# Windowed attention with block summaries and two feed-forward layers: batch 0's keys and value sums loaded in 4-row and 2-row runs by half of the heads, softmax by pairs of heads, and another order of the work

## The chip, the cores and the metric

One core of one Trainium2 chip. The metric is the device time of one launch in microseconds (us), the median of the runs shown; less is better.

## The reference, cut to what matters

```python
# q, k, v: 2 batches x 8 heads x 768 tokens x 64, float32
block, window = (32, 16)
k_sum = k.reshape(B, H, nb, block, D).max(axis=3)     # 24 summaries per head
v_sum = v.reshape(B, H, nb, block, D).mean(axis=3)
scores_l = scale * q @ k.T, kept where |i - j| < 16
scores_s = scale * q @ k_sum.T + log(32)
a = softmax over [scores_l, scores_s]
x = a @ [v, v_sum]             # 1536 tokens x 512
h = x @ w_in;  x = relu(h)**2 @ w_out           # layer 0: 512 -> 2048 -> 512
h = x @ w_in2; out = h * sigmoid(1.702 * h) @ w_out2    # layer 1: 512 -> 2048 -> 512
```

The weights are float64 in memory (8 bytes each), q, k and v float32.

## The kernel before, in words

**Tiling.** Attention works on blocks of 128 tokens: six of batch 0 (blocks 0 to 5), six of batch 1. q and k come in units of 256 tokens (two blocks) through SyncE's DMA queue (`load_unit`, L374). A "packed" unit puts two consecutive tokens on one partition, so that DMA reads runs of 512 bytes; an unpacked one reads runs of 256 bytes. TensorE transposes a unit against an identity (`transposed`, L462, four 128x128 transposes per PSUM bank at L473), and ScalarE or VectorE copies the bank to `kw` or `qT` (`copy`, L309 on ScalarE, L310 on VectorE). For keys (`t_k`, L488) VectorE takes the maximum of every 32 tokens (L502), GpSimd copies 16-token edges between neighbouring blocks (L509), and when all three units of a batch are there `put_ks` (L518) copies the 24 summaries beside each block's keys (L523). So no block of batch 0 can be scored before all of its keys have landed. The value sums (`sum_v`, L438) are matmuls with a band matrix (L452) over all 768 tokens; `put_vs` (L418) puts them beside the value windows `vw` (`load_vw`, L398: 80 or 96 partitions, runs of 256 bytes).

**One block.** `head` (L534) issues the 16 score matmuls of all eight heads (64x64 tiles, L551; the trace shows each as two), VectorE scales and masks each head and takes its maximum (L565), ScalarE does the exponentials of the four even, then of the four odd heads (L574), GpSimd or VectorE adds 1e-9 (L578), VectorE takes the reciprocal (L588), and VectorE or GpSimd multiplies (L581). `tail` (L593) transposes the result (L602), copies it (`pT`), multiplies with `vw` (L614) and splits the sum into a high and a low part `xh` (L309 or L310) and `xl` (L627).

**Layers.** `fetch` (L684) loads 128 columns of `w_in` (L690) or 128 rows of `w_out` (L694), half a megabyte each, and turns float64 into float32 (L699, L703, L706); `parts` splits that into a high part (L730 or L731) and a low part (L735). `step` (L757) issues the first product of one column group (L768) for 256 or 512 tokens, `finish` (L808) the second (L820).

**Order.** Nothing is ordered by the hardware alone: the string `ORDER` lists tasks (`k,2,1` loads unit 2 of k packed, `tk`, `tq` transpose, `h,i,e` and `t,i` are head and tail of block i, `w,f,z` prepares half of a weight group, `s,f,hf` is a step on 256 tokens, `S,f` on 512), and `Plan` places each operation at its planned start on its engine and emits all by it. `Plan.fill` puts `warm` matmuls (L1123), whose result nobody reads, into the planned gaps of TensorE until the accumulator bank `acc3` is first written.

The line that decides when the layers may begin is the read list of a step:

```python
op("PE", 0.682 * fr + (0.018 if fr < 1 else 0), g1,
   reads=[(wih, 0), (wil, 0)] + [(x[t], (kc, b)) for x in (xh, xl) for b in blks], writes=[(hp, 0)])
```

A step on 256 tokens waits for `xh` and `xl` of two blocks and for the two parts of its weights.

Of the kernel before, what the change touches and what calls it, by code (L numbers as in the profile page):

```python
# [19 lines left out]
NEG = -8.0e9  # L20

# [6 lines left out]
    m,1 k,2,1 sel w,1,0 m,0 k,1,1 q,1,1 k,0,1 tk,0 tk,1 tk,2 pk,0 q,0,1 sv,0 tq,0 h,1,0 tq,1 m,2 h,1,1 h,0,0  # L28
    w,1,1 pk,1 q,2,0 v,0 h,0,1 ps,0 h,3,0 tq,2 v,1 t,1 h,2,0 v,2 v,3 pk,2 h,2,1 t,0 h,3,1 k,3,0 t,2 s,1,0
    t,3 tk,3 w,2,0 q,3,0 tq,3 k,4,1 tk,4 w,3,0 h,4,0 s,1,1 w,3,1 h,5,0 s,3,0 k,5,0 s,3,1 w,5,0 h,5,1 w,2,1  # L30
    w,0,0 q,4,1 s,2,0 tk,5 w,5,1 S,5 w,9,0 s,2,1 w,6,0 h,4,1 pk,3 w,9,1 v,4 S,9 w,6,1 pk,5 tq,4 w,0,1 t,4
    v,5 h,7,0 w,7,0 s,0,0 t,5 w,7,1 s,0,1 w,4,0 S,7 q,5,1 w,11,0 pk,4 w,4,1 h,6,0 sv,1 S,4 h,7,1 v,6 ps,1
    w,8,0 w,11,1 tq,5 v,7 t,7 S,6 h,6,1 w,10,0 h,8,0 v,8 S,11 h,9,0 h,8,1 t,6 w,8,1 h,9,1 v,9 v,10 w,15,0
    t,8 S,8 w,10,1 S,10 w,12,0 w,12,1 w,15,1 v,11 t,9 h,10,0 w,13,0 S,12 S,15 w,14,0 h,11,0 w,13,1 h,10,1
    S,13 w,14,1 h,11,1 t,10 S,14 t,11
# [220 lines left out]
def kernel(  # L256
# [73 lines left out]
    consts = Buf([], None)  # L330

# [32 lines left out]
    kw_ring = ring(attn, "kw", 4, [P, NPAIR, 2, KW])  # L364
# [12 lines left out]
    def load_unit(dst, src, ring_, u, packed):  # L377
        b, j = divmod(u, NU)
        buf = ring_.take()
        if packed:  # L380
            plan.dma(1.85, lambda: nc.sync.dma_start(
                out=buf.t.rearrange("p (h r d) -> p h r d", h=H, r=2),
                in_=src[b, :, j * UNIT:(j + 1) * UNIT, :].rearrange("h (p r) d -> p h r d", r=2)), writes=[(buf, 0)])
# [77 lines left out]

    def transposed(src, dst):  # L462
# [4 lines left out]
        for n in range(2):  # L467
            ps = banks.take()

            def go(n=n, ps=ps):  # L470
                for a in range(4):
                    c0 = (2 * a + n) * P if packed else (a % 2) * H * D + (2 * n + a // 2) * P
                    nc.tensor.transpose(ps.t[:, a * P:(a + 1) * P], buf.t[:, c0:c0 + P], ident)  # L473

            op("PE", 0.46, go, reads=[(buf, 0), (consts, "ident")] + ([] if packed else [(buf, 1)]), writes=[(ps, 0)])
            if not packed:
                copy(lambda n=n: at(slice(0, P), slice(2 * n, 2 * n + 2)),
                     lambda ps=ps: ps.t.rearrange("p (a i t) -> p a i t", a=2, i=2), ps, [(w, ("own", 2 * n))])
                w.writer["own", 2 * n + 1] = plan.ops[-1]
                continue  # L480
            for i in range(2):
                copy(lambda n=n, i=i: at(slice(n * D, n * D + D), slice(0, NPAIR)).rearrange(
                    "p a z (t i) -> p a z t i", i=2)[:, :, :, :, i],
                     lambda ps=ps, i=i: ps.t[i * D:i * D + D, :].rearrange("p (a z t) -> p a z t", a=4, z=2),
                     ps, [(w, ("own", 2 * n + i))], cost=0.59)

    OWNS = [("own", x) for x in range(4)]

    def t_k(u):
# [5 lines left out]
        zero = [(0, NSUM)] if j == 0 else [(1, OWN + P)] if j == NU - 1 else []  # L495
        for i, c0 in zero:
            op("POOL", 0.2, lambda i=i, c0=c0: nc.gpsimd.memset(w.t[:, :, i, c0:c0 + EDGE], 0.0),
               writes=[(w, (i, "l" if c0 == NSUM else "r"))])
        transposed(kin[u], (w, lambda rows, ps: w.t[rows, ps, :, OWN:OWN + P]))
        for z in range(2):  # L500
# [4 lines left out]
               reads=[(w, x) for x in (OWNS if kin[u][1] else OWNS[2 * z:2 * z + 2])], writes=[(ks[b], (j, z))])  # L505
        R = OWN + P

        def edge(dst, di, d0, src, si, s0, side):
            op("POOL", 0.22, lambda: nc.gpsimd.tensor_copy(  # L509
                out=dst.t[:, :, di, d0:d0 + EDGE], in_=src.t[:, :, si, s0:s0 + EDGE]),  # L510
               reads=[(src, x) for x in OWNS], writes=[(dst, (di, side))], port=True)
# [23 lines left out]
    def head(i, e):  # L535
# [5 lines left out]
        if e == 0:  # L541
            both = [banks.take()]
            both.append(banks.take(both[0]))
            sms[i] = sm_ring.take(), st_ring.take()

            def mm():
                for p in range(NPAIR):
                    for c in range(2):
                        k0 = c * (KW - NK)
                        for x in range(2):  # L550
                            nc.tensor.matmul(  # L551
                                both[x].t[c * HALF:(c + 1) * HALF, p * NK:(p + 1) * NK],
                                lhsT=qt.t[x * D:(x + 1) * D, p, z * P + c * HALF:z * P + (c + 1) * HALF],
                                rhs=w.t[x * D:(x + 1) * D, p, z, k0:k0 + NK],
                                start=True, stop=True,
                            )

            op("PE", 0.98, mm, reads=[(w, (z, "l")), (w, (z, "r")), (w, ("s", 0)), (w, ("s", 1))]
               + [(x, y) for x in (w, qt) for y in OWNS], writes=[(both[0], 0), (both[1], 0)])
        s, st = sms[i]  # L560
        for x in range(2 if e == 0 else 0):
            def mx(x=x):
                for p in range(NPAIR):
                    h = 2 * p + x
                    nc.vector.tensor_tensor_reduce(  # L565
                        out=s.t[:, h, :], in0=both[x].t[:, p * NK:(p + 1) * NK], in1=mk, scale=-SCALE, scalar=3.0e38,
                        op0=ALU.add, op1=ALU.min, accum_out=st.t[:, 0, h:h + 1],
                    )

            op("DVE", 0.87, mx, reads=[(both[x], 0), (consts, ("mask", mi))], writes=[(s, x), (st, (0, x))])  # L570

        def ex(e=e):
            for h in range(e, H, 2):
# [583 lines left out]
```

## Time and profile before

| | |
|---|---|
| median of 3 runs | 587.07 us (586.4 to 587.27) |
| span of the profiled execution | 584.6 us |
| TensorE busy | 571.6 us, 98% of the span |
| VectorE, ScalarE, GpSimd busy | 480.4, 441.8, 65.8 us |
| TensorE granted clock | full in all 40 slices |
| first layer step (L768) starts | 36.18 us |

The time of a launch holds the span and about 2.5 us around it (587.07 against 584.6). A share of busy time is an average: the span has an opening, where TensorE has little of its own to do and runs fillers, and the rest, where it hardly pauses. A matmul's shown end is modelled; starts are what shows the pace. A float32 matmul appears as two records, a float32 transpose as one.

### The profile page before, as it was taken

To read this page: it belongs to the slowest core of one execution; us is meant where nothing else is said; L and a number is where in the kernel's file an instruction comes from. 1 tells how busy PE (TensorE), PEld (TensorE's weight loads), DVE (VectorE), ACT (ScalarE), POOL (GpSimd) and SP (SyncE) were. 2 spreads that over 40 slices of the span, in tenths; PEclk is the share of its full clock that TensorE was granted. 3 is DMA by queue.
4 is the path that set the end of the run, shared out by engine and by line. 5 is a ranking of instruction groups with operands and counts; after the bars stand their busy time and mean duration, and the time that the engine had idled before them with its cause. 6 is when DMAs were issued, how large, how long until landed. Compare 5 with 4: busy or idle time off the path is not lost.

```text
span 584.6 us, 9824 instructions
## 1 busy us (share of the span) xinstructions
PE 571.6 (98%) x3440; PEld 474.3 (81%) x3440; DVE 480.4 (82%) x1040; ACT 441.8 (76%) x909; POOL 65.8 (11%) x125
## 2 busy tenths in 40 slices
PE   7899999999999999999999999999999999999997
PEld 6789888788878888888888888888878888888885
DVE  4899998799889998878888899899998898877421
ACT  5899889999888658888888867676587777778322
POOL 5323113112100000100000000000100002000000
PEclk9999999999999999999999999999999999999999
DMA  9999889555446624444444546633465455545001
GB/s 251 238 237 239 243 260 255 148 172 180 148 148 191 201 71 143 143 145 145 145 145 143 180 145 211 186 112 104 148 181 177 152 178 174 178 163 200 0 1 72
DMA packets 87505, 95.79 MB, mean 164 GB/s; under 512 B 29504, under 2 KB 74560, under 8 KB 87456
## 3 DMA queue, kind: packets, MB, share of 16 engines
q1 hardware_dynamic: 87264, 94.78, 54.1%
q0 software_dynamic: 192, 0.39, 0.4%
q8 instruction: 27, 0.44, 0.3%
q14 instruction: 22, 0.18, 0.1%
HBM read 91.62 MB, written 3.15 MB: 162 GB/s over the span
## 4 chain that ended last, share of the span: by engine, by line
PE 86%; ACT 5%; DVE 4%; DMA 3%; SPq 1%; issue 1%; POOL 0%; DVEq 0%; ACTq 0%
PE acc L996 13%; PE acc L820 13%; PE acc L822 11%; PE m L996 10%; PE m L822 9%; PE h L768 6%; PE m L820 6%; PE h L996 3%; PE acc L768 3%; PE m L768 3%; PE h L822 3%; PE h L820 2%; ACT sm L574 2%; PE m L614 2%; DMA kin<-in_k_dram 1%; DMA kin<-in_v_dram 1%
## 5 line engine op out<-in xcount | busy, mean ns | idle before, releaser
L730 ACT CAST w<-xw 128x512 fp32r<-128x512 f32 (+1 forms) x167 | 97.9, 602 | 20.1 <-DVE xw L706 12.8
L735 DVE TENSOR_TENSOR w<-xw,w 128x512 fp32r<-128x512 f32 (+1 forms) x163 | 107.5, 672 | 5.9 <-ACT w L730 4.0
L706 DVE SCALAR_TENSOR_TENSOR xw<-raw,xw 128x512 uint32<-128x512 uint32 x148 | 101.5, 695 | 5.6 <-ACT raw L699 1.8
L699 ACT ACTIVATE raw<-raw 128x512 f32<-128x512 f32 x148 | 96.1, 675 | 10.9 <-DMA raw<-in_moe_w_out_dram 6.3
L820 PE MATMUL acc<-gh,w 128*128 128x512 f32 (+1 forms) x288 | 82.3, 369 | 0.4 <-DVE w L735 0.2
L703 DVE TENSOR_SCALAR xw<-raw 128x512 uint32<-128x512 uint32 x148 | 65.8, 449 | 6.2 <-DMA raw<-in_moe_w_out_dram 5.8
L820 PEld LDWEIGHTS acc<-gh,w 128*128 128x128 f32 x288 | 51.7, 188 | 9.9 <-DVE w L735 0.5
L822 PE MATMUL acc<-w,gh 128*128 128x512 f32 x192 | 59.1, 389 | 0.0
L768 PE MATMUL h<-xh,w 128*128 128x512 f32 (+1 forms) x184 | 55.6, 363 | 0.6 <-DVE st L588 0.6
L820 PE MATMUL acc<-gl,w 128*128 128x512 f32 (+1 forms) x144 | 52.7, 366 | 0.0
L996 PE MATMUL acc<-top,w 128*128 128x512 f32 x192 | 48.3, 391 | 0.0
L822 PE MATMUL m<-w,gh 128*128 128x512 f32 x148 | 45.7, 390 | 0.0
L735 DVE TENSOR_TENSOR gl<-gs,gh 128x512 fp32r<-128x512 f32 x32 | 22.1, 691 | 28.5 <-ACT gh L730 27.8
L730 ACT CAST gh<-gs 128x512 fp32r<-128x512 f32 x32 | 19.9, 622 | 33.5 <-PE acc L822 25.4
L735 POOL TENSOR_TENSOR w<-xw,w 128x512 fp32r<-128x512 f32 x17 | 22.9, 1344 | 195.9 <-ACT w L730 170.2
L996 PEld LDWEIGHTS acc<-top,w 128*128 128x128 f32 x192 | 35.8, 188 | 8.5 <-ACT r L309 1.2
L822 PEld LDWEIGHTS acc<-w,gh 128*128 128x128 f32 x192 | 36.0, 188 | 7.5
L768 PEld LDWEIGHTS h<-xh,w 128*128 128x128 f32 x184 | 33.3, 189 | 6.3 <-ACT sm L574 0.8
L822 PE MATMUL acc<-w,gl 128*128 128x512 f32 x96 | 37.4, 389 | 0.0
L574 ACT ACTIVATE sm<-sm,st 128x120 f32<-128x120 f32 x96 | 36.6, 383 | 0.0
L996 PE MATMUL m<-top,w 128*128 128x512 f32 x138 | 35.0, 391 | 0.0
L996 PE MATMUL acc<-xh,w 128*128 128x512 f32 x100 | 34.0, 389 | 0.0
(188 smaller groups left out, 1201.8 us busy)
## 6 DMA issues: line engine op xcount, KB each, us to landing
raw<-in_moe_w_out_dram SPq DMA_DIRECT2D x88, 512.0 KB, 3.8
raw<-in_moe_w_in_dram SPq DMA_DIRECT2D x60, 512.0 KB, 3.9
vw<-in_v_dram SPq DMA_DIRECT2D x20, 192.0 KB, 5.8
kin<-in_v_dram SPq DMA_DIRECT2D x6, 512.0 KB, 7.0
out_dram<-r SPq DMA_DIRECT2D x12, 256.0 KB, 2.1
kin<-in_k_dram SPq DMA_DIRECT2D x4, 512.0 KB, 6.0
qin<-in_q_dram SPq DMA_DIRECT2D x4, 512.0 KB, 7.1
qin<-in_q_dram SPq DMA_DIRECT2D x4, 256.0 KB, 6.8
```

The source lines that it names most:

```text
L574: nc.scalar.activation(out=s.t[:, h, :], in_=s.t[:, h, :], func=AF.Exp, bias=st.t[:, 0, h:h + 1], scale=-1.0, accum_out=st.t[:, 1, h:h + 1])
L614: nc.tensor.matmul(ps.t[e * D:(e + 1) * D, p * P + c * HALF:p * P + (c + 1) * HALF], lhsT=vw[i].t[:, c, h * D:(h + 1) * D], rhs=t.t[:, h, ...
L699: nc.scalar.activation(out=top, in_=top, func=AF.Prelu, scale=-(2.0 ** -80), alpha=-(2.0 ** -32))
L703: op("DVE", 0.36, lambda: nc.vector.tensor_scalar(out=x.t, in0=raw.t[:, :, 0], scalar1=29, scalar2=None, op0=ALU.logical_shift_right), rea ...
L706: op("DVE", 0.64, lambda: nc.vector.scalar_tensor_tensor(out=x.t, in0=raw.t[:, :, 1], scalar=3, in1=x.t, op0=ALU.logical_shift_left, op1=A ...
L730: plan.soonest([("ACT", 0.09 + 0.44 * fr, False, lambda: nc.scalar.copy(out=hi.t[:, hc], in_=src())), ("DVE", 0.05 + 0.4 * fr, True, lambd ...
L735: eng.tensor_tensor(out=lo.t[:, lc], in0=src(), in1=hi.t[:, hc].bitcast(F32), op=ALU.subtract)
L768: nc.tensor.matmul(hp.t[:, cols], lhsT=w.t[:, kc * P:(kc + 1) * P], rhs=x.t[:, kc, cols], start=(kc == 0 and n == 0), stop=(kc == KC - 1 a ...
L820: nc.tensor.matmul(a.t[:, cols], lhsT=w.t[:, j * P:(j + 1) * P], rhs=g.t[:, cols], **st)
L822: nc.tensor.matmul(a.t, lhsT=g.t[:, j * P:(j + 1) * P], rhs=w.t, **st)
L996: nc.tensor.matmul(bank.t, lhsT=a, rhs=rhs(b, kh), start=(begin and k == 0 and n == 0), stop=(k == 1 and n == 2), skip_group_check=True)
```

## The change

Batch 0's keys no longer come as three units of 256 tokens with all heads. For each half of the heads there is a load of tokens 0 to 511 with four consecutive tokens on a partition (1,024-byte runs, `load_long`) and one of tokens 512 to 767 with two (512-byte runs, `load_short`). `t_kp` transposes one pair of heads with 64-column matmuls against the identity (L588 after the change; 12 per pair), which leaves the pair's two heads on partitions 0 to 63 and 64 to 127, then reduces, copies edges and puts the summaries for that pair at once, in all six blocks. The value sums of batch 0 use the same two kinds of load (`sum_v0`). A softmax now takes two pairs of heads (heads 0 to 3, then 4 to 7) in place of even and odd heads, and `head_half` scores a block by such halves. Unit 2 of q may be loaded by halves of the heads (`packed == 2`). The order string is another one. The layers' code is unchanged but for names; so is the count of their matmuls.

```diff
 ORDER = """
-    m,1 k,2,1 sel w,1,0 m,0 k,1,1 q,1,1 k,0,1 tk,0 tk,1 tk,2 pk,0 q,0,1 sv,0 tq,0 h,1,0 tq,1 m,2 h,1,1 h,0,0
...
+    K,0 B,0 q,0,1 m,2 selw T,0 m,1 tq,0 K,1 B,1 q,1,1 q,3,0 T,3 T,1 T,2 tq,1 m,0 g,1,0 V,0 g,1,1 v,0 V,1
+    g,0,1 V,2 g,0,0 h,2,0 v,1 ps,0 t,1 w,2,0 h,2,1 h,3,0 q,2,2 t,0 w,2,1 tq,2 w,1,0 h,3,1 v,2 v,3 s,2,0
...
-    kw_ring = ring(attn, "kw", 4, [P, NPAIR, 2, KW])
+    kw_all = attn.tile([P, NPAIR, 8, KW], F32, tag="kw", name="kw")
+    kw_ring = Ring(4, lambda i: kw_all[:, :, 2 * i:2 * i + 2, :])
...
+    def load_long(src, g):
+        buf = kin_ring.take()
+        hs = slice(4 * g, 4 * g + 4)
+        plan.dma(1.45, lambda: nc.sync.dma_start(
+            out=buf.t.rearrange("p (h x) -> p h x", h=4),
+            in_=src[0, hs, 0:LONG].rearrange("h (p r) d -> p h (r d)", r=4)), writes=[(buf, 0)])
+        return buf
+
+    def load_short(src, buf, gs):
+        h0, h1 = 4 * gs[0], 4 * gs[-1] + 4
+        plan.dma(0.95 if len(gs) == 1 else 1.85, lambda: nc.sync.dma_start(
+            out=buf.t.rearrange("p (h x) -> p h x", h=H)[:, h0:h1],
+            in_=src[0, h0:h1, LONG:S].rearrange("h (p r) d -> p h (r d)", r=2)), writes=[(buf, g) for g in gs])
...
+        def go():
+            x = buf.t.rearrange("p (h r d) -> p h r d", h=2 * len(ps), r=run)
+            for r in range(run):
+                for n, p in enumerate(ps):
+                    nc.tensor.matmul(acc_v.t[32 * p:32 * p + NSUM, 0:P], lhsT=bands[i // 2],
+                                     rhs=x[:, 2 * n:2 * n + 2, r, :], start=(first and r == 0), stop=(i == 2 and r == 1))
...
+    def t_kp(p):
...
+            def go(buf=buf, h0=h0, run=run, ps=ps):
+                for r in range(run):
+                    for x in range(2):
+                        c0 = ((h0 + x) * run + r) * D
+                        nc.tensor.matmul(ps.t[x * D:(x + 1) * D, r * P:(r + 1) * P], lhsT=buf.t[:, c0:c0 + D],
+                                         rhs=ident, start=True, stop=True)
...
+        rd = every(("own", p, 0))
+        op("DVE", 0.87, lambda: nc.vector.tensor_reduce(
+            out=ks[0].t[:, p, :].rearrange("p (j n) -> p j n", j=NB),
+            in_=mine(OWN, OWN + P).rearrange("p j (n t) -> p j n t", t=BLK), axis=AX.X, op=ALU.max),
+           reads=rd, writes=[(ks[0], ("p", p))])
...
-    def head(i, e):
+    def scores(i, gs):
...
+        ps = [p for g in gs for p in (2 * g, 2 * g + 1)]
...
+    def softmax(i, g):
+        s, st = sms[i]
+        hs = slice(4 * g, 4 * g + 4)
...
+            for h in range(4 * g, 4 * g + 4):
...
+    def head_half(i, g):
+        scores(i, (g,))
+        softmax(i, g)
```

**SyncE's queue, opening, before.** The rows are DMA issues in program order; `kin` holds k or v, `qin` q, `raw` weights, `vw` value windows, and the last column is partitions x runs x elements.

```order
L381 DMA kin_98<-in_k_dram 128x8x128
L690 DMA raw_107<-in_moe_w_in_dram 128x4x256
L381 DMA kin_128<-in_k_dram 128x8x128
L381 DMA qin_164<-in_q_dram 128x8x128
L381 DMA kin_179<-in_k_dram 128x8x128
L381 DMA qin_205<-in_q_dram 128x8x128
L444 DMA kin_219<-in_v_dram 128x8x128
L444 DMA kin_236<-in_v_dram 128x8x128
L444 DMA kin_267<-in_v_dram 128x8x128
```

**The same after the change.** Two loads of k, the first half of the heads, stand ahead of these rows.

```order
L396 DMA qin_117<-in_q_dram 128x8x128
L417 DMA kin_147<-in_k_dram 128x4x256
L424 DMA kin_106<-in_k_dram 128x4x128
L396 DMA qin_193<-in_q_dram 128x8x128
L403 DMA qin_222<-in_q_dram 128x8x64 x2
L417 DMA kin_270<-in_v_dram 128x4x256
L452 DMA vw<-in_v_dram 80x8x64
L452 DMA vw<-in_v_dram 96x8x64
L417 DMA kin_354<-in_v_dram 128x4x256
L424 DMA kin_385<-in_v_dram 128x8x128
L452 DMA vw<-in_v_dram 96x8x64 x2
L832 DMA raw_442<-in_moe_w_in_dram 128x4x256
```

The first weight load moves from the second place to the fourteenth, behind all of k, q, v and the first windows; q of batch 1 (`qin_222`, unit 3) comes ahead of v.

**TensorE, opening, before.** `warm` are the fillers; `kin_98`, `kin_128`, `kin_179` are the three units of k.

```order
L1123 MATMUL warm<-ident 128x128 x7
L473 MATMUL m_130<-ident,kin_98 128x128 x4
L473 MATMUL m_135<-ident,kin_98 128x128 x4
L1123 MATMUL warm<-ident 128x128 x6
L473 MATMUL acc_183<-ident,kin_128 128x128 x4
L473 MATMUL h_190<-ident,kin_128 128x128 x4
L1123 MATMUL warm<-ident 128x128 x6
L473 MATMUL acc_221<-ident,kin_179 128x128 x4
L473 MATMUL acc_227<-ident,kin_179 128x128 x4
```

**The same after the change.** `kin_85` and `kin_147` are the long loads of the two halves of the heads, `kin_106` the short ones.

```order
L1283 MATMUL warm<-ident 128x128 x6
L588 MATMUL acc_122<-ident,kin_85 64x128 x8
L588 MATMUL acc_149<-ident,kin_106 64x128 x4
L588 MATMUL m_155<-ident,kin_85 64x128 x8
L542 MATMUL acc_173<-ident,qin_117 128x128 x4
L542 MATMUL h_195<-ident,qin_117 128x128 x4
L588 MATMUL acc_204<-ident,kin_106 64x128 x4
L588 MATMUL m_211<-ident,kin_147 64x128 x8
L588 MATMUL m_225<-ident,kin_106 64x128 x4
L588 MATMUL acc_233<-ident,kin_147 64x128 x8
L588 MATMUL m_248<-ident,kin_106 64x128 x4
```

24 transposes have become 48 matmuls of 64 columns, in fours and eights per bank, and the fillers between them are gone; over the whole program there are 14 fillers where there were 40.

**ScalarE after the change**, from the first exponential to the second block's `xh`; `sm` is a block's softmax, of block 1 (`sm_294`), 0 (`sm_341`) and 2 (`sm_407`).

```order
L707 ACTIVATE sm_294,st_295<-sm_294,st_295 128x120 x8
L707 ACTIVATE sm_341,st_342<-sm_341,st_342 128x120 x8
L310 COPY pT_428<-acc_394 120x512
L310 COPY pT_428<-h_422 120x512
L310 COPY vs_464<-m_345 24x128 x3
L707 ACTIVATE sm_407,st_408<-sm_407,st_408 128x120 x4
L464 COPY vw<-vs_464 24x512 x2
L841 ACTIVATE raw_442<-raw_442 128x512
L310 COPY pT_529<-h_484 120x512
L310 COPY pT_529<-m_491 120x512
L310 CAST xh_537<-m_510 128x4x128
L707 ACTIVATE sm_407,st_408<-sm_407,st_408 128x120 x4
```

Before, two scalings (L699) and two casts (L730) of weights stood on ScalarE ahead of its first `xh` cast; now one scaling stands there, and the cast that belongs to it is VectorE's.

## Rows read from the trace of the kernel before

**Rows 1.** The profile's page: busy time of the engines, granted clock by slices.
```profile
PE 571.6 (98%) x3440; PEld 474.3 (81%) x3440; DVE 480.4 (82%) x1040; ACT 441.8 (76%) x909; POOL 65.8 (11%) x125
...
PEclk9999999999999999999999999999999999999999
```

**Rows 2.** Stretches: busy us (instructions) of PE, PEld, DVE, ACT, POOL; clock; DMA share, GB/s.
```profile
0.00:36.18 36.18, 28.30 (x389) 24.77 (x389) 25.54 (x104) 27.39 (x83) 14.18 (x58) 1.00 1.06 238
36.18:60.00 23.82, 23.58 (x282) 21.97 (x283) 21.78 (x69) 22.52 (x70) 8.14 (x18) 1.00 0.92 247
60.00:130.00 70.00, 69.09 (x654) 57.77 (x653) 61.39 (x171) 63.22 (x165) 14.70 (x23) 1.00 0.77 213
130.00:580.00 450.00, 449.95 (x2118) 369.64 (x2117) 371.66 (x698) 327.45 (x594) 28.77 (x26) 1.00 0.45 145
```

**Rows 3.** Timeline of TensorE: units of k arriving, first scores, first layer step.
```profile
5.05 1.18 PE L473 MATMUL m<-ident,kin 128*128 128x128 f32 x8 [0.27 <-DMA kin<-in_k_dram]
...
11.99 1.09 PE L473 MATMUL acc<-ident,kin 128*128 128x128 f32 x8 [1.18 <-DMA kin<-in_k_dram]
...
36.18 0.35 PE L768 MATMUL h<-xh,w 128*128 128x256 f32 x1 [0.62 <-DVE st L588]
```

**Rows 4.** Timeline of ScalarE: the first exponential, the first `xh`.
```profile
20.92 0.39 ACT L574 ACTIVATE sm<-sm,st 128x120 f32<-128x120 f32 x1
...
33.40 0.58 ACT L309 CAST xh<-m 128x512 fp32r<-128x512 f32 x1 [0.29 <-PE m L614]
```

**Rows 5.** The same windows view, for DMA in the opening and two thin stretches of TensorE.
```profile
3.00:6.00 3.00, 2.73 (x17) 2.44 (x16) 0.00 (x0) 0.17 (x1) 2.48 (x15) 1.00 1.12 342
6.00:18.00 12.00, 9.06 (x101) 7.75 (x98) 9.58 (x17) 10.03 (x17) 3.94 (x19) 1.00 1.22 292
22.00:32.00 10.00, 8.12 (x94) 7.18 (x93) 8.84 (x46) 9.80 (x42) 4.49 (x10) 1.00 1.11 188
10.00:12.00 2.00, 0.82 (x9) 0.63 (x7) 1.97 (x4) 1.06 (x2) 0.68 (x4) 1.00 1.22 290
28.00:30.00 2.00, 0.94 (x9) 0.74 (x7) 1.82 (x12) 1.95 (x4) 1.69 (x2) 1.00 1.21 176
```

**Rows 6.** Timeline of TensorE: a filler, band sums, and column-tiled products, by start.
```profile
9.30 1.50 PE L1123 MATMUL warm<-ident 128*128 128x128 f32 x12
...
15.76 0.64 PE L452 MATMUL m<-kin,band 128*24 128x128 f32 x16
...
32.20 1.15 PE L614 MATMUL m<-pT,vw 120*64 120x64 f32 x32
33.18 1.12 PE L614 MATMUL h<-pT,vw 120*64 120x64 f32 x32
```

**Rows 7.** Groups by line and form in 0 to 36.2 us: busy us, mean ns.
```profile
L574 ACT ACTIVATE sm<-sm,st 128x120 f32<-128x120 f32 x27 | 10.3, 382 | 0.0
L502 DVE TENSOR_REDUCE ks<-kw 128x16 f32<-128x512 f32 x6 | 3.8, 681 | 0.8 <-ACT kw L309 0.7
L581 DVE TENSOR_TENSOR sm<-sm,st 128x480 f32<-128x480 f32 x4 | 2.6, 658 | 0.8 <-ACT sm L574 0.5
L309 ACT COPY qT<-m 64x512 f32<-64x512 f32 x4 | 2.5, 626 | 0.1
L523 DVE COPY kw<-ks 128x192 f32<-128x192 f32 x6 | 1.2, 256 | 0.1
L627 DVE TENSOR_TENSOR xl<-h,xh 128x512 fp32r<-128x512 f32 x1 | 0.7, 692 | 0.0
L309 ACT COPY vs<-m 24x128 f32<-24x128 f32 x3 | 0.8, 257 | 1.8 <-PE m L452 1.4 <-DVE vs L310 0.4
L309 ACT COPY pT<-m 120x512 f32<-120x512 f32 x1 | 0.6, 569 | 0.0
```

**Rows 8.** Chain of work that ended last, 0 to 48 us: start, us, what.
```profile
21.01 4.54 ACT sm L574 x24
```

**Rows 9.** What TensorE waited for, 0 to 130 us: total, times, longest.
```profile
PE m L602 <- DVE xl L627: 0.5, 1, 0.5
```

More of the change, by code (lines that the diff above doesn't have):

```diff
@@ L330, with make_bands @@
     consts = Buf([], None)
+    LONG = 4 * P
+    bands = [attn.tile([P, NSUM], F32, tag=f"band{i}", name=f"band{i}") for i in range(2)]
+    def make_bands():
+        for i, (run, n0) in enumerate(((4, 0), (2, LONG // BLK))):
+            per = BLK // run
+            nc.gpsimd.memset(bands[i], 1.0 / BLK)
+            nc.gpsimd.affine_select(out=bands[i], in_=bands[i], pattern=[[-per, NSUM]], compare_op=ALU.is_ge,
+                                    fill=0.0, base=per * n0, channel_multiplier=1)
+            nc.gpsimd.affine_select(out=bands[i], in_=bands[i], pattern=[[per, NSUM]], compare_op=ALU.is_ge,
+                                    fill=0.0, base=per - 1 - per * n0, channel_multiplier=-1)
     def make_ident():
@@ L481, in transposed @@
[L481 to L487, printed above, removed]
+                    if packed < 2:
+                        c0 = (2 * a + n) * P if packed else (a % 2) * H * D + (2 * n + a // 2) * P
+                        nc.tensor.transpose(ps.t[:, a * P:(a + 1) * P], buf.t[:, c0:c0 + P], ident)
+                        continue
@@ L510, in edge @@
                 out=dst.t[:, :, di, d0:d0 + EDGE], in_=src.t[:, :, si, s0:s0 + EDGE]),
-               reads=[(src, x) for x in OWNS], writes=[(dst, (di, side))], port=True)
+               reads=own(src), writes=both(dst, (di, side)), port=True)
         edge(w, 0, R, w, 1, OWN, "r")
@@ L540, in head @@
         qt, w = qT[u], kw[u]
-        if e == 0:
-            both = [banks.take()]
-            both.append(banks.take(both[0]))
+        both = [banks.take()]
+        both.append(banks.take(both[0]))
+        if i not in sms:
             sms[i] = sm_ring.take(), st_ring.take()
[L546 to L559, printed above, removed]
@@ L676, in layer @@
                 prep(m, f)
-            step(m, t, f, 0, TT, [n == 0] * 2, [n == len(order) - 1] * 2)
+            step(m, t, f, 0, TT, [fresh and n == 0] * 2, [n == len(order) - 1] * 2)
             if n >= 2:
@@ L1100 @@
     end_attention()
+    if not mores:
+        drain()
+    early.clear()
     plan.lean = 1.5, 0.25
     banks.release(banks.last["h0"])
-    while pending:
-        finish()
     parted.add((0, 0))
@@ L1108 @@
     two = list(range(NF))
-    layer(1, 0, two[:1:-1][:10], operands_first(0, 1, 2, *one[:2]))
+    rest = [f for f in two[:1:-1] + two[1::-1] if f not in mores]
+    layer(1, 0, rest[:-BACK], operands_first(0, 1, 2, *one[:2]), not mores)
     pairs(0, 1, 2, one)
@@ L1112 @@
     keep_w.update({(1, two[0]), (1, two[1])})
-    layer(1, 0, two[:1:-1][10:] + two[1::-1], operands_first(1, 2, 1, *two[:2]))
+    layer(1, 0, rest[-BACK:], operands_first(1, 2, 1, *two[:2]))
     pairs(1, 2, 1, two)
```

210 lines of the change are left out of this document (157 added, 53 removed).

## The prediction

> **What bounds the kernel now.** I read the page first: TensorE is busy 98% of the span at full clock throughout [rows 1]. A share over the whole span hides stages, so next come the stretches [rows 2]. From 130 to 580 us TensorE is busy 449.95 of 450 us; from 60 to 130 it is 69.09 of 70, from 36.18 to 60 it is 23.58 of 23.82. Nothing can be won there without fewer matmuls, and the change leaves the layers' count alone. The opening is different. The first layer step starts at 36.18 us [rows 3], and much of the 28.3 us that TensorE shows busy before it [rows 2] is fillers: 12 of their records take 1.50 us, 0.11 from start to start [rows 6], and there are 80 of them. So the kernel's time is the start of the layers, plus the TensorE work left at that moment, plus what TensorE waits afterwards. Three views show what sets that start: k's last unit reaches TensorE at 11.99 [rows 3], the first exponential runs at 20.92 and the first `xh` at 33.40 [rows 4], and from 22 to 32 us ScalarE is busy 9.80 of 10 us, VectorE 8.84 [rows 5]. The start is set by k's arrival and then by ScalarE's line of work.
>
> **The landings.** The first unit of k is first in the queue and is used at 5.05, the third is fifth and is used at 11.99 [rows 3]: 1.74 us per half megabyte. After the change k takes places worth 1, 0.5, 1 and 0.5 such units with q's first unit between them. The second long load lands after 3.5 units, at 5.05 + 2.5 x 1.74 = 9.4; all of k after 4 at 10.3; q's second unit after 5 at 12.0.
>
> The rate itself is not one number: 342 GB/s from 3 to 6 us, where a w_in load with 1,024-byte runs is among the transfers, 292 from 6 to 18 with 512-byte runs almost alone, 188 from 22 to 32 with many 256-byte runs [rows 5]. At 342 a half megabyte takes 1.53 us, at 292 it takes 1.80. If the new 1,024-byte loads go at the first rate, the two ahead of q save 0.5 us, and the result would be 583.8; my sum takes 1.74 for all. The Trainium skill ("DMA: Bandwidth & Descriptors", Specifications) gives 512 B as the least transfer for line rate; by that the longer runs gain nothing and the sum stays at 584.3.
>
> **Transposes of k.** 48 matmuls of 64 columns replace 24 transposes, and 16 more replace 8 for q's third unit. Each is two records of 0.11 us. What they cost depends on whether two column halves run side by side. The nearest row is the product with `vw`, whose output halves also stand on different partitions: 32 records of 64 moving columns start within 0.98 us, 0.031 each [rows 6], half of what 0.11 for 128 columns would give in single file. So a pair costs 0.23 us; 64 matmuls take 7.4 us against 3.7. The band sums of the two long loads use two column groups in place of four: 0.92 each against 0.6 [rows 6]. These 4.3 us replace fillers. The second half of the heads needs 8 + 4 + 8 + 4 matmuls, 2.8 us, from 9.4 to 12.2, and q's transposes 0.9 more, to 13.1.
>
> **To the first exponential.** Behind the last bank: a copy of 256 columns, 0.35 (from 0.626 for 512 [rows 7]), to 12.6. A maximum over 768 elements, 1.0 us (0.681 for 512 [rows 7]), to 13.6. Two summary copies of at most 0.256, to 14.1; edges run on GpSimd beside them. VectorE masks block 1 from 14.2. ScalarE has four q copies in between, 4 x 0.626, from 12.7 to 15.2, and starts its exponentials there: 5.7 us before 20.92.
>
> **From there to `xh`, on ScalarE in its new order.** Twelve exponentials took 4.54 us, 0.378 each [rows 8]. Sixteen take 6.1, to 21.3; two `pT` copies 1.1, to 22.4. The copies of the value sums need v's third load. Queue after 12.0: q of batch 1 (256-byte runs, 2.8 at 188 GB/s), a long v load 1.8, two windows of 0.36 MB 1.9, two v loads 3.6: 22.1, and 0.7 for the band sums. So three copies of 0.257 from 22.8, to 23.6. Four exponentials, to 25.1; two copies to `vw` 1.2, a weight scaling 0.7, two `pT` copies 1.1, to 28.1; the `xh` cast 0.6, to 28.7. Before it ended at 33.98.
>
> **To the first step.** In the old trace 2.2 us lie between that end and the step [rows 3, 4]. Now the next four exponentials (1.5) and a normalisation with reciprocal (about 1.0, [rows 7]) are ahead of the second `xl` (0.69) on VectorE: 28.7 + 1.5 + 1.0 + 0.7 = 31.9, the step at 32.0. It needs w_in, now fourteenth in the queue: 22.1 + 2.1 (windows) + 1.8 = 26.0, and 3.3 us of scaling and splitting end by 29.3, hidden. The gain here is **4.2 us**.
>
> **After the first step.** Four more L602 transposes are already done by then, 0.4 us less left. Against that, work waits sooner for weights. Behind the step stand 16 score matmuls, one product, four transposes: TensorE is done at 32.0 + 1.4 + 1.0 + 1.1 + 0.5 = 36.0. The second group's w_in lands three units later, near 31.2, but its cast and low part stand behind seven ScalarE and five VectorE pieces and end near 36.9. One such wait of 0.9, and another of 0.9 where block 3's product needs its `pT` after four exponentials: 1.8 us, where the old trace has only one wait of 0.5 in that place [rows 9] and 0.24 us idle to 60 us [rows 2]. I keep 1.8 as loss. Later stages have 0.9 us idle from 60 to 130 and a slack of about a tenth on both other engines [rows 2]; I leave them at no change.
>
> **The sum.** -4.2 - 0.4 + 1.8 = -2.8 us on the profiled span, 584.6 to 581.8. The median of the runs is 587.07, 2.5 us above that span; the same 2.5 gives **584.3**. Bounds of this case: no new waits and the faster loads, -5.1; exponentials 2 us later, -0.8.
>
> **The rivals.**
> - *ScalarE and VectorE eat the gain.* From 36.18 to 60 us they are busy 22.52 and 21.78 of 23.82 [rows 2]; a start 4 us sooner needs the same feeding sooner, and 1.3 us of slack on ScalarE does not give 4. For it: TensorE never waits there now because it started late. Against it: the change takes copies from ScalarE (twelve copies of about 0.62 for k become four of 512 and some of 256 columns). It gives 586.5, from 585.5 to 587.5. Chance 0.15.
> - *Weights late: slower.* If everything behind q's second unit moves at 188 GB/s, 3.4 MB end at 30.0 in place of 26.0 and the step starts at 33.3. Worse, three more half megabytes take 8.4 us, so the second group is ready near 41.8, where TensorE's own work ends at 37.3; 4.5 us of wait, and some 2 for the next group. -2.9 - 0.4 + 6.5 = +3.2, 590.3. It decides once w_in lands later than 29. For it: window loads of 256-byte runs stand between v and the weights. Against: the v loads are long runs. Chance 0.13.
> - *Halves in single file.* The 48 matmuls take 11 us and ScalarE's exponentials start 5 us later: +2.2, 589.3. Against it the row on the product. Chance 0.05.
> - *The clock falls.* 26 fillers are gone, and from 13 to 28 us TensorE has some 8 us of its own work. The trace has stretches as thin, 0.82 of 2 us and 0.94 of 2, at full clock [rows 5], though short. At 1.2 GHz the two products, the transposes and the first step, about 4 us on the path, would double: 588.3. Chance 0.05. The Trainium skill ("TensorE: Matmul & The Clock Gate", Part 1) says that idleness halves the clock and activity restores it; no stretch of this trace shows the lower level.
>
> **How the numbers follow.** The forecast keeps 0.62. About 0.2% (1.2 us) is what a measurement here can tell from no change: faster is below 585.9, slower above 588.2. Faster: 0.59 of the forecast, 0.04 of the first rival, 0.01 of the clock: 0.64. Same: 0.03, 0.09, 0.02 of the weights, 0.03 of clock and single file: 0.17. Slower: the rest, 0.19. The range 581.0 to 588.5 holds nearly all of the forecast, the first rival and most of the clock's case, 0.8 together; the forecast's own range is 582.0 to 586.3.
>
> **What would show it.** Right: the first exponential near 15, the first `xh` near 28.5, the first layer step near 32, granted clock full, and TensorE idle 1 to 2 us more between 32 and 60. Two records of half-width transposes every 0.11 us. Wrong: a step at 34 or later; a wait of TensorE for weights of over 3 us in sum; records of the k transposes at 0.11 each in single file; a clock below full; or a changed busy sum after 130 us, which I take as fixed.

## The result and the profile after

| | before | changed |
|---|---|---|
| median of the runs | 587.02 us (586.4 to 587.27) | 581.54 us (581.38 to 582.38) |
| ratio | | 0.9904, 95% interval 0.9885 to 0.9923 |
| span of the profiled execution | 584.6 us | 579.9 us |
| TensorE's last matmul starts | 580.25 us | 575.18 us |
| last product with the values starts | 161.37 us | 156.30 us |
| first layer step starts | 36.18 us | 33.97 us |

Faster, by 5.5 us where 2.7 were forecast: inside the range, near its lower end, and below the forecast's own range of 582.0 to 586.3. The changed kernel was run once more beside later experiments: 582.01 us. In the traces all of the gain is there by the last product with the values, the last work of the attention: 5.07 us, as at the last matmul. The traces show 4.7 to 5.1 us where the medians show 5.5: an execution's time stands 1.7 to 1.8 us above its own span (581.62 against 579.9), not 2.5, so that the traced execution of the kernel before took some 586.4 us, less than its median.

The page after, which answers to [rows 1]:

```profile
PE 568.5 (98%) x3484; PEld 472.1 (81%) x3484; DVE 476.6 (82%) x1035; ACT 435.8 (75%) x905; POOL 65.3 (11%) x130
...
PEclk9999999999999999999999999999999999999999
```

The stretches after, cut at the new first step, with the columns of [rows 2]:

```profile
0.00:33.97 33.97, 27.47 (x436) 23.32 (x436) 22.47 (x100) 26.57 (x88) 15.49 (x64) 1.00 1.04 253
33.97:60.00 26.03, 25.49 (x302) 24.46 (x303) 23.84 (x70) 22.21 (x61) 7.06 (x11) 1.00 0.88 230
60.00:130.00 70.00, 70.00 (x676) 58.45 (x675) 62.01 (x174) 62.63 (x170) 14.87 (x30) 1.00 0.84 223
130.00:575.00 445.00, 445.00 (x2075) 365.71 (x2072) 368.28 (x693) 323.32 (x588) 27.87 (x26) 1.00 0.45 145
```

From 60 us to 575 TensorE doesn't pause at all; before it paused 0.91 us from 60 to 130. Its timeline after, against [rows 3]: k's first half, the last half-width group of q's unit 2, and the first layer step with what it waited for.

```profile
4.87 1.65 PE L588 MATMUL acc<-ident,kin 128*64 128x128 f32 x24 [0.51 <-DMA kin<-in_k_dram]
6.36 1.04 PE L588 MATMUL m<-ident,kin 128*64 128x128 f32 x16
...
30.23 1.07 PE L546 MATMUL h<-ident,qin 128*64 128x128 f32 x16
...
33.97 0.39 PE L911 MATMUL h<-xh,w 128*128 128x256 f32 x1 [0.75 <-ACT qT L310]
```

ScalarE's timeline after, against [rows 4]: the first exponential, the first `xh`, and the pieces ahead of that step.

```profile
15.16 0.39 ACT L707 ACTIVATE sm<-sm,st 128x120 f32<-128x120 f32 x1
...
28.67 0.61 ACT L310 CAST xh<-m 128x512 fp32r<-128x512 f32 x1
...
32.19 0.68 ACT L841 ACTIVATE raw<-raw 128x512 f32<-128x512 f32 x1
...
33.27 0.65 ACT L310 COPY qT<-h 128x256 f32<-128x256 f32 x2
```

The first step takes the bank `h` that held unit 2 of q; ScalarE's copies that empty it stand behind eight exponentials and a weight scaling. The transfers after, against [rows 5]:

```profile
3.00:6.00 3.00, 2.49 (x25) 2.19 (x25) 0.00 (x0) 0.00 (x0) 2.41 (x15) 1.00 1.13 339
6.00:12.00 6.00, 5.84 (x91) 5.13 (x88) 4.54 (x9) 4.62 (x9) 3.61 (x18) 1.00 1.18 315
12.00:22.00 10.00, 8.29 (x150) 6.58 (x150) 8.61 (x53) 9.67 (x39) 1.95 (x10) 1.00 1.19 252
22.00:32.00 10.00, 8.19 (x163) 6.95 (x162) 7.52 (x36) 9.02 (x33) 5.24 (x9) 1.00 1.10 278
```

**How far ahead is it at 45 us?** TensorE's groups by line and form from 0 to 45 us count the work done by then. Before:

```profile
L551 PE MATMUL acc<-kw,qT 64*64 64x120 f32 x84 | 4.4, 269 | 1.9 <-ACT qT L309 1.1 <-issue 0.8
L551 PE MATMUL m<-kw,qT 64*64 64x120 f32 x48 | 2.1, 269 | 0.0
L551 PE MATMUL h<-kw,qT 64*64 64x120 f32 x16 | 1.0, 269 | 0.0
L768 PE MATMUL h<-xh,w 128*128 128x256 f32 x8 | 1.9, 301 | 0.6 <-DVE st L588 0.6
L768 PE MATMUL h<-xl,w 128*128 128x256 f32 x4 | 1.1, 282 | 0.0
```

After:

```profile
L677 PE MATMUL m<-kw,qT 64*64 64x120 f32 x88 | 5.2, 271 | 0.0
L677 PE MATMUL acc<-kw,qT 64*64 64x120 f32 x88 | 4.8, 269 | 0.0
L911 PE MATMUL h<-xh,w 128*128 128x256 f32 x16 | 3.4, 293 | 0.7 <-ACT qT L310 0.7
L911 PE MATMUL h<-xl,w 128*128 128x256 f32 x8 | 2.3, 282 | 0.0
L963 PE MATMUL acc<-gh,w 128*128 128x256 f32 x6 | 1.3, 311 | 0.0
L963 PE MATMUL acc<-gl,w 128*128 128x256 f32 x3 | 0.8, 282 | 0.0
L677 PE MATMUL h<-kw,qT 64*64 64x120 f32 x16 | 1.2, 269 | 0.0
```

Score records: 192 against 148, 44 more at 0.031 us from start to start: 1.4 us. Layer records: 33 against 12, 21 more at 0.12: 2.5 us. The kernel before had in turn transposed two units of batch 1's k by then (16 records at 0.11, 1.8 us), the changed one none. Products, transposes of the softmax, band sums and q's units are equal in number. So the changed kernel is **2.1 us ahead at 45 us**, and the other **3.0 us come between 45 and 161 us**.

There the view of waits gives nothing for the changed kernel, and for the kernel before four (45 to 165 us; total, times, longest):

```profile
PE m L602 <- DVE xl L627: 0.5, 1, 0.5
PE acc L820 <- DVE w L735: 0.2, 1, 0.2
PE m L602 <- DVE st L588: 0.2, 1, 0.2
PE acc L820 <- DVE st L565: 0.2, 1, 0.2
```

They show 1.1 us. From start to start, less the usual pace of the same record, the four gaps (at 50, 66, 81 and 117 us) cost 1.8 of the 3.0; the rest is spread over many gaps of under 0.2 us.

### The profile page after: what moved, and what is told of

It is laid out like the page before. It is cut to its first block, busy times and chain, and to the rows that moved or that the text cites. A ratio compares the mean times of both kernels' runs of the same rounds, so it can differ in the third digit from the quotient of the medians.

```text
span 579.9 us, 9905 instructions
## 1 busy us (share of the span) xinstructions
PE 568.5 (98%) x3484; PEld 472.1 (81%) x3484; DVE 476.6 (82%) x1035; ACT 435.8 (75%) x905; POOL 65.3 (11%) x130
## 4 chain that ended last, share of the span: by engine, by line
PE 93%; DMA 2%; ACT 2%; DVE 1%; SPq 0%; issue 0%; DVEq 0%
PE acc L963 15%; PE acc L1139 13%; PE acc L965 11%; PE m L965 9%; PE h L911 9%; PE h L1139 7%; PE m L1139 6%; PE m L963 6%; PE acc L911 3%; PE m L911 2%; PE h L965 2%; PE h L963 2%; PE m L756 1%; PE m L744 1%; DMA kin<-in_v_dram 1%; PE m L677 1%
## 5 line engine op out<-in xcount | busy, mean ns | idle before, releaser
L877 DVE TENSOR_TENSOR w<-xw,w 128x512 fp32r<-128x512 f32 (+1 forms) x169 | 112.8, 678 | 7.9 <-ACT w L872 4.3
L845 DVE TENSOR_SCALAR xw<-raw 128x512 uint32<-128x512 uint32 x148 | 63.8, 436 | 3.4 <-DMA raw<-in_moe_w_out_dram 2.7
L911 PE MATMUL h<-xh,w 128*128 128x512 f32 (+1 forms) x192 | 57.8, 364 | 0.7 <-ACT qT L310 0.7
L965 PE MATMUL m<-w,gh 128*128 128x512 f32 x160 | 49.4, 390 | 0.0
L1139 PE MATMUL acc<-top,w 128*128 128x512 f32 x186 | 47.1, 391 | 0.0
L911 PEld LDWEIGHTS h<-xh,w 128*128 128x128 f32 x192 | 34.6, 189 | 6.2 <-ACT qT L310 0.9
L965 PEld LDWEIGHTS m<-w,gh 128*128 128x128 f32 x160 | 30.0, 188 | 6.5 <-ACT gh L940 0.4
L877 POOL TENSOR_TENSOR w<-xw,w 128x512 fp32r<-128x512 f32 x11 | 14.8, 1349 | 181.3 <-ACT w L872 158.8
L911 PE MATMUL h<-xl,w 128*128 128x512 f32 (+1 forms) x96 | 34.0, 355 | 0.0
```

Source lines behind the costliest of these rows:

```text
L845: op("DVE", 0.36, lambda: nc.vector.tensor_scalar(out=x.t, in0=raw.t[:, :, 0], scalar1=29, scalar2=None, op0=ALU.logical_shift_right), rea ...
L877: eng.tensor_tensor(out=lo.t[:, lc], in0=src(), in1=hi.t[:, hc].bitcast(F32), op=ALU.subtract)
L911: nc.tensor.matmul(hp.t[:, cols], lhsT=w.t[:, kc * P:(kc + 1) * P], rhs=x.t[:, kc, cols], start=(kc == 0 and n == 0), stop=(kc == KC - 1 a ...
L965: nc.tensor.matmul(a.t, lhsT=g.t[:, j * P:(j + 1) * P], rhs=w.t, **st)
L1139: nc.tensor.matmul(bank.t, lhsT=a, rhs=rhs(b, kh), start=(begin and k == 0 and n == 0), stop=(k == 1 and n == 2), skip_group_check=True)
```

## The experiments

A median is compared with the kernel before on the same chip (587.18 us for the first four, 587.17 for the next four, 587.20 for the three after, 586.81 for the last). Where the order string is changed the plan is made anew, and with it the choice of ScalarE or VectorE for copies and casts: such a run changes more than its title says.

**Old order, new softmax.** The changed program with the order string of the kernel before, so with the old loads; only the softmax by two pairs of heads is new.

```diff
-    K,0 B,0 q,0,1 m,2 selw T,0 m,1 tq,0 K,1 B,1 ...
+    m,1 k,2,1 sel w,1,0 m,0 k,1,1 q,1,1 k,0,1 tk,0 ...
```

> The changed program with the old order string: keys and value sums of batch 0 are loaded and transposed as in the kernel before, and only the softmax works on two pairs of heads instead of even and odd heads. Theory A (loads and order carry the gain): within 0.8 us of the kernel before, near 587.0, first layer step near 36 us. Theory B (the softmax by pairs carries what TensorE stopped waiting for after the first step, about 2 us): near 585.0, step still near 36 us.

588.23 us, ratio 1.0021 (1.0007 to 1.0034). First exponential at 21.71, first `xh` at 34.16, first layer step at 40.29, 4.1 us later than before. The median is only 1 us longer, but the traced execution took 590.58 us, with a span of 588.6: in it the end is 4.0 us later too. The plan had put the second block's `xh` on ScalarE behind eight exponentials (37.68), where VectorE did it at 34.63 before. The softmax by pairs brings nothing with the plan that came with it.

**New loads, old order.** The old order string with its tasks for batch 0's k and v replaced.

```diff
-    k,2,1 ... k,1,1 ... k,0,1 ... tk,0 tk,1 tk,2 pk,0 ... sv,0
+    K,0 B,0 selw ... K,1 ... B,1 ... T,0 T,1 T,2 T,3 ... V,0 V,1 V,2
```

> The old order string with only batch 0's k and v tasks replaced: long and short loads by halves of the heads, 64-column transposes, value sums from long and short runs; the first w_in load stays early and q, tails, weights and steps stand as before. Theory A1 (the loads themselves bring the gain, because k's transposes, maxima and summaries end sooner): first exponential near 17 to 19 us, first step 34 to 35 us, total near 585. Theory A2 (the new order brings it): first step 36 us or later, total 587 or more, since the transposes cost TensorE 3 us more.

590.1 us, ratio 1.0045 (1.0028 to 1.0062). First exponential at 22.93. The transposes of k's first half are done by 8.5 us, but its last load is used only at 11.61, 0.4 us sooner than in the kernel before, since weights and a unit of q stand ahead of it; and this order has nothing use what is early: in the chain of waits the first exponentials stand behind a v load that lands at 19.97, the copies of the value sums and one to `vw`. TensorE pays for the longer transposes and gets nothing back. Another placing of the new loads in the old order wasn't tried. TensorE's first step and last matmul:

```profile
44.82 0.39 PE L904 MATMUL h<-xh,w 128*128 128x256 f32 x1 [0.17 <-DVE xl L762]
...
584.12 0.39 PE L958 MATMUL acc<-w,gl 128*128 128x512 f32 x1
```

The step is 8.6 us later than before, the last matmul 3.9: the start of the first step doesn't measure the kernel.

**New order, old loads.** The new order string with the old three units of k and the old value sums.

```diff
-    K,0 B,0 ... selw T,0 ... K,1 B,1 ... T,3 T,1 T,2 ... V,0 ... V,1 ... V,2
+    k,0,1 k,1,1 ... sel tk,0 ... k,2,1 ... tk,1 tk,2 pk,0 pk,1 pk,2 ... sv,0
```

> The new order string with batch 0's keys loaded, transposed and summarised by 256-token units of all heads, and value sums from 512-byte runs, as before the change. Theory A1 (loads bring the opening's gain): first exponential 18 us or later, first step near 36 us, total near 586 to 587. Theory A2 (the order brings it, weights and activations meeting TensorE better after the step): step near 35 us and total 583 to 585, with TensorE's waits after the step as small as in the changed kernel.

588.74 us, ratio 1.0022 (1.0008 to 1.0037). TensorE's timeline of this run at the first scores:

```profile
17.93 0.43 PE L670 MATMUL m<-kw,qT 64*64 64x120 f32 x1 [4.16 <-DVE kw L639]
```

and two of its stretches, columns as in [rows 2]:

```profile
12.00:18.00 6.00, 1.84 (x18) 1.68 (x18) 4.62 (x10) 4.95 (x9) 1.36 (x7) 0.87 1.15 278
18.00:22.80 4.80, 4.80 (x81) 3.73 (x81) 3.15 (x28) 3.90 (x19) 0.22 (x1) 0.50 1.30 215
```

With units of all heads the first scores wait for every summary, 4.16 us; and the granted clock is 0.50, 1.2 GHz, from 16.5 us, within that idle time, to 23.3. So this run mixed two things, and the last one below takes them apart.

**The bank sooner.** The changed kernel with its plan kept, and the two copies that empty the first step's bank moved ahead of the scaling.

```diff
+    ops = {o.seq: o for o in plan.ops}
+    for n in (166, 167):
+        ops[n].start = ops[157].start - 1e-3
     with tc.manual_schedule():
         plan.emit()
```

> The changed kernel, with nothing planned anew: on ScalarE the two copies that empty the accumulator bank of the first layer step (second half of q's third unit) go ahead of one weight scaling and of the two other q copies. Theory C (the start of the layers sets the end): the first step moves from 33.97 to about 32.8 us, where the second block's low part is ready, and the total falls by about 1.1 us to 580.4. Theory D (after the step TensorE waits for what ScalarE and VectorE feed, so a sooner start is given back): step near 32.8 us, total within 0.4 us of 581.5, and TensorE idle about 1 us more between 33 and 45 us.

582.13 us, ratio 0.9912 (0.9891 to 0.9933): no gain. Its TensorE timeline has the first step 1.1 us sooner and a longer wait 7 us later, where the changed kernel shows 0.54, at 40.28:

```profile
32.86 0.36 PE L911 MATMUL h<-xh,w 128*128 128x256 f32 x1
...
40.13 0.62 PE L744 MATMUL m<-ident,sm 128*120 128x128 f32 x4 [1.17 <-DVE sm L714]
```

**The v loads sooner.** The changed kernel, plan kept, with the two loads of q's unit 3 issued behind the first weights.

```diff
+    ops = {o.seq: o for o in plan.ops}
+    for n in (27, 28):
+        ops[n].start = ops[148].start + 1e-3
```

> The changed kernel with its plan kept, and the two loads of unit 3 of q (batch 1, half a megabyte, ahead of the first load of v in the changed kernel) behind the first weight load and unit 2 of q. The changed kernel's chain of waits goes through the first load of v (landing at 22.38 us) to the value sums, the first two products with the values and the cast of xh at 28.67. Half a megabyte at the 250 GB/s of 12 to 22 us is 2.1 us, so v should land 1 to 2 us sooner and the cast start at 27 to 28 in any case. Theory that the v load's landing sets the end: the time falls by 1 to 2 us, to 579.7 to 580.7. Rival (the opening is now held by ScalarE's and VectorE's work for the first two steps and by banks, not by a transfer, as when the bank came free sooner): 581.2 to 582.0, the idle time of TensorE before 45 us the same 15 us, only elsewhere.

580.90 us, ratio 0.9896 (0.9883 to 0.9908); span 579.0. In the changed kernel the band sums waited three times for v:

```profile
17.00 1.06 PE L518 MATMUL m<-kin,band 128*24 128x128 f32 x16 [1.18 <-DMA kin<-in_v_dram]
...
20.38 1.06 PE L518 MATMUL m<-kin,band 128*24 128x128 f32 x16 [0.53 <-DMA kin<-in_v_dram]
...
22.42 0.64 PE L518 MATMUL m<-kin,band 128*24 128x128 f32 x16 [0.40 <-DMA kin<-in_v_dram]
```

Here they don't wait:

```profile
15.76 1.06 PE L518 MATMUL m<-kin,band 128*24 128x128 f32 x16
...
19.00 1.06 PE L518 MATMUL m<-kin,band 128*24 128x128 f32 x16
...
20.58 0.64 PE L518 MATMUL m<-kin,band 128*24 128x128 f32 x16
```

The third starts 1.84 us sooner, but the cast of `xh` (27.85) and the first step (33.16) only 0.8: the copies of the value sums now stand behind ScalarE's exponentials and `pT` copies, which end at 22.4. The span is 0.9 us shorter. The median lies between the two theories, 0.2 us above the first's 579.7 to 580.7 and 0.3 below the rival's: v's landing is a limit, but ScalarE's line takes half of what it gives.

**The later order put back.** The changed order up to and with its second step, then the tasks left in the order of the kernel before.

```diff
-    w,3,1 k,3,0 s,2,1 s,1,1 s,3,1 s,3,0 w,6,0 ...
+    k,3,0 tk,3 k,4,0 tk,4 s,1,1 w,3,1 h,5,0 s,3,0 ...
```

> The changed kernel's order up to and with its second layer step (group 1, first half), and from there the remaining tasks in the order of the kernel before. Theory that the opening alone brings the gain: 581.5 to 582.2, and TensorE idle after 45 us no longer than in the changed kernel. Theory that some 2.5 us of the 5.5 come from the later order (after 45 us TensorE of the kernel before loses about 2.5 us more than that of the changed one): 583.5 to 584.5, with waits of TensorE between 45 and 165 us that the changed kernel doesn't have.

583.54 us, ratio 0.9943 (0.993 to 0.9956). Up to 45 us TensorE's work is the changed kernel's; the last product starts at 157.57, 1.27 later (0.9 later than in the changed kernel's second trace, 156.64), and a wait for weights is back ("PE acc L956 <- DVE w L870", 0.3 us) in the only stretch after 45 us that isn't full:

```profile
60.00:130.00 70.00, 69.69 (x660) 58.73 (x659) 61.24 (x171) 59.08 (x152) 13.33 (x20) 1.00 0.83 218
```

So the later order carries 1.0 to 1.2 us by the spans (581.1 against 580.1 and 579.9) and 1.5 to 2.0 by the medians. The rest of the 3.0 us after 45 us stays with the old later order too: it comes with what this run and the changed kernel share, the new opening and the softmax by pairs. Which of the two wasn't tried apart.

**Nine fillers more, in both kernels.** At one place, behind the first matmuls of the first layer step.

```diff
+    first = next(o for o in plan.ops if o.fn.__qualname__.endswith("step.<locals>.g1"))
+    for n in range(9):
+        o = Op()
+        o.eng, o.fn, o.seq, o.far, o.start = "PE", keep_warm, len(plan.ops), False, first.start + 1e-3
+        plan.ops.append(o)
```

> The changed kernel with its plan kept and nine more fillers (18 matmul records, at 0.115 to 0.125 us each 2.1 to 2.2 us) on TensorE right behind the first matmuls of the first layer step, at about 34 us. Theory that from there on TensorE's own work sets the end and nothing else: +2.1 to +2.2 us, 583.6 to 583.8. Rival (the waits for ScalarE and VectorE that follow, as the 0.5 us for the third block's softmax at 40 us, absorb a delay): +0.5 to +1.5, 582.0 to 583.0. If the feeding engines set the pace of the whole stretch to 130 us: +0 to +0.3.

> The kernel before with its plan kept and the same nine fillers at the same place, behind the first matmuls of its first layer step (36.2 us). If TensorE's own work sets the end: +2.1 to +2.2, 589.1 to 589.4. It shows waits of its own from 36 to 130 us (0.24 us idle to 60, 0.91 from 60 to 130, and slower pacing beside them), so less should arrive than in the changed kernel if those waits are for other engines: +1.0 to +1.8, 588.0 to 588.9. The difference between the two runs of fillers is the part of the change's later gain that comes from waits which a later start would have hidden.

The timeline shows what was added in the kernel before, 1.92 us from the fillers' start to the next matmul:

```profile
36.71 2.17 PE L1123 MATMUL warm<-ident 128*128 128x128 f32 x18
38.63 0.36 PE L768 MATMUL h<-xh,w 128*128 128x256 f32 x1
```

Changed kernel: 582.86 us, 0.9 to 1.3 more than its two medians, span 1.8 more; the 0.54 us wait for the softmax at 40 us is gone. Kernel before: 588.67 us, 1.5 more, span 1.3 more; of its four waits after 45 us the one for weights, 0.2 us, is gone. Most of a delay arrives at the end and some is absorbed by a later wait, in both alike. That the kernel before would swallow more of it than the changed one wasn't seen, so a later start explains little of the later gain.

**Both moves together**, the v loads' and the bank's.

```diff
+    ops = {o.seq: o for o in plan.ops}
+    for n in (27, 28):
+        ops[n].start = ops[148].start + 1e-3
+    for n in (166, 167):
+        ops[n].start = ops[157].start - 1e-3
```

> The changed kernel with its plan kept and both moves together: unit 3 of q behind the first weight load, and the two copies that empty the bank of the first layer step ahead of a weight scaling on ScalarE. With the v load sooner the cast of xh came 0.8 us sooner and so did the first layer step (33.16), which then still waited 0.8 us for that bank. Theory that the gain of the v load was held by the bank: the step at 32.3 to 32.6 and 580.0 to 580.6. Rival (the third block's softmax on VectorE is the next limit, as it was when the bank alone was freed): the step sooner, a longer wait of TensorE for the softmax at 38 to 41 us, and 580.7 to 581.3, no gain over the v load's move alone.

580.77 us (580.7 to 581.54), ratio 0.9891 (0.9871 to 0.9912), span 579.0. The step starts at 32.17, and nothing further is gained over the v loads' move: the rival's time held, and its limit, though not its longer wait. The transposes that need the third block's softmax start at 39.47, against 39.45 with the v loads' move alone, after waits of 0.56 and 0.52 us; what the step gained stands in a pause of 0.58 us before some scores at 35.19.

**No fillers**, and **the changed kernel again**, on the same chip:

```diff
-    plan.fill(0.27, keep_warm, first_ops["acc3"])
```

> The changed kernel without its 14 fillers. Theory that they only fill TensorE's idle time and that the clock doesn't need them: 581.2 to 581.9, granted clock 2.4 GHz (1.00) in the stretch from 5 to 60 us. Rival that TensorE's clock depends on them: 1.2 GHz granted in some stretch of the opening, the 48 matmuls of the key transposes there at 0.11 us a record in place of 0.056 and the time 583 to 588. If the fillers stand in the way of work that is ready: 580.0 to 581.0.

> The changed kernel itself, unedited, beside the others on the same chip, as the measure for the moves of the v load: 581.3 to 582.0. If the v load's move is worth what its trace shows (span 0.9 us shorter), the changed kernel stands 0.5 to 1.0 us above the 580.9 of that run; if it was the spread between executions, less than 0.3.

The changed kernel gave 582.01 us (581.8 to 583.29), so both moves are worth 1.2 us beside it, with runs that don't overlap; this is the fastest version. Without fillers it was 583.11 us, 1.1 more. TensorE's timeline there:

```profile
4.99 2.83 PE L588 MATMUL acc<-ident,kin 128*64 128x128 f32 x24 [4.99 <-DMA kin<-in_k_dram]
7.57 1.95 PE L588 MATMUL m<-ident,kin 128*64 128x128 f32 x16
```

24 records take 2.58 us, 0.108 each, where the changed kernel takes 1.49, 0.062 each. `xh` is 1.8 us later, as is the first step (35.81).

**New order, old loads, TensorE kept busy.** The third run above with 14 fillers in its idle 4.16 us.

```diff
+    first = min((o for o in plan.ops if o.fn.__qualname__.endswith("scores.<locals>.mm")), key=lambda o: o.start)
+    for n in range(14):
+        o = Op()
+        o.eng, o.fn, o.seq, o.far, o.start = "PE", keep_warm, len(plan.ops), False, first.start - 1e-3
+        plan.ops.append(o)
```

> The run of the new order with the old loads of k and v, its plan kept, and 14 fillers (28 records, 3.1 us at 0.11) in the 4.16 us in which TensorE stood idle there before the first scores. In that run the granted clock was 0.50 (1.2 GHz) from 18 to 22.8 us, right after that idle time. Theory that the new order alone would have gained and that the fallen clock hid it: the clock at 1.00 throughout, the first exponential at 19.6 or somewhat sooner, and at least 2.4 us (half of those 4.8) off its 588.74: 586.3 or less, down to 585. Rival (the order needs the new loads, since the first scores still wait for all summaries, at 17.9): the clock at 1.00 too, but ScalarE's line of work starts at the same place and the time stays at 587.5 to 588.8.

587.20 us, ratio 1.0002 (0.999 to 1.0014). The same stretch now, at full clock:

```profile
18.00:22.80 4.80, 4.49 (x130) 3.67 (x130) 4.49 (x36) 4.37 (x19) 0.23 (x2) 1.00 1.03 202
```

The fallen clock had cost 1.2 us by the ratios to the kernel before, 1.5 by the medians, which are of two chips; the new order alone is then level with the kernel before. The first exponential stays at 19.55, since its keys come no sooner. The later order is the changed kernel's here, yet TensorE pauses 0.92 us from 60 to 130 us, as before the change:

```profile
60.00:130.00 70.00, 69.08 (x632) 57.49 (x631) 63.14 (x188) 61.51 (x167) 15.05 (x30) 1.00 0.84 225
```

So with the old loads the later order doesn't take these pauses away.

## Why the prediction was half right

**Right: the mechanism of the opening.** The first exponential ran at 15.16 (forecast 15.2), the `xh` cast ended at 29.28 (28.7). TensorE waited for k only once, 0.5 us. The halves ran side by side: 0.062 us a record against the 0.0575 worked out. The faster rate for longer runs was partly so: 315 GB/s from 6 to 12 us, between the 292 and the 342 of [rows 5]. The Trainium skill ("DMA: Bandwidth & Descriptors", Specifications) gives 512 B as enough for line rate; these rows don't bear out that longer runs gain nothing, though they don't show the run length as the cause: the stretch with 1,024-byte runs moved some 8% more than one of 512-byte runs, with other transfers among them in both.

**Off: the first step.** "The step at 32.0" became 33.97, at the edge of the sign of being wrong. I followed `xl` and the weights (VectorE's `xl` was done at 32.66) and missed the PSUM bank. It cost nothing that could be won back there, as the run with the bank sooner shows. The sum was made from the step's start, but other work of TensorE fills the time before it; the run with the step at 44.82 shows how little that start says. What counts is the work done by a later moment: 2.1 us more by 45 us, where the terms of the opening, the step and its waits together gave 2.8. That the two are near is partly luck: the step brought 2.2 us in place of 4.2, the waits charged at 1.8 came to 0.3 (0.54 from the step to 60 us, against 0.24), and the two errors have opposite signs.

**Wrong: "Later stages have 0.9 us idle from 60 to 130 ...; I leave them at no change."** This is the step that failed. It was worth 3.0 us. I had [rows 2] show 0.24 and 0.91 us idle after the first step and took them as given, though the diff says that the order string is another one throughout. The changed kernel has no wait from 45 us on. Part of that, 1.0 to 2.0 us, is the later order, shown by putting the old one back; with the old loads that order leaves pauses of 0.92 us from 60 to 130 us. The rest came with the new opening and the softmax by pairs. What makes the small gaps fewer there wasn't tried, so the cause of that part stays open.

**The rivals.** ScalarE and VectorE did not eat the gain: from 33.97 to 60 us ScalarE was busy 22.21 of 26.03, and TensorE waited once for the softmax, 0.54 us, in place of the two waits of 0.9 that I charged. Weights were never late: no wait of TensorE there names one. The clock stayed at 1.00, but not for want of a mechanism: it fell in the run with the old loads, and without the first fillers TensorE's opening runs at half its pace. I wrote that no stretch of the old trace shows the lower level. Its clock column doesn't, but its first 14 filler records take 3.35 us, where 12 later ones take 1.50 [rows 6].

**What makes the gain** is loads and order together. Loads alone (with the new softmax, as placed here): 2.9 us slower. Order alone: 1.6 slower, and level with the clock kept up. Both: 5.5 faster. Keys that are ready pair by pair helped only where scores, exponentials and value sums were ordered to use them, and that order stalls on keys that come for all heads at once.

## What to carry to other kernels

When a change rewrites an order, price each wait of the old timeline that the new order might remove, also far behind the place the change is about; here the stretch from 45 to 161 us showed 1.1 us of waits and gave 3.0 us. Don't take the start of a stage as the measure where the busy engine has other work to do: count what it has done by a later moment. Test loads and order apart before crediting one of them.

## What the runs showed of the hardware

The granted clock of TensorE stood at 0.50 (1.2 GHz) from 16.5 to 23.3 us in the run where TensorE had stood idle for 4.16 us up to 17.93, and stayed at 1.00 with fillers there. In the run without fillers the clock column says 1.00 in every stretch, yet the first 40 matmul records went at half their usual pace, after 4.99 us without a matmul, and at 11.37 the pace was the usual one (24 records in 1.31 us). The Trainium skill ("TensorE: Matmul & The Clock Gate", Part 1) says that the gate starts at half rate and that activity opens it; the pace agrees, 0.108 us a record against 0.062, and the column doesn't. By then the run is 2.3 us behind the changed kernel, where the same records start at 9.09; at the end 1.1 us of it are left. The changed kernel starts at the low pace too, but there it falls on fillers, 0.21 us from start to start:

```profile
1.44 2.93 PE L1283 MATMUL warm<-ident 128*128 128x128 f32 x12 [1.44 <-POOL ident masks.py:199]
```

The pace of the rows, not the column, tells a slow start.
